# Gate, exponential and sine tiles of the second pair of chunks kept in the space of w2 and h, and a new order of the first thousand operations

## The chip, the core and the metric

The kernel runs on one core of a Trainium2 chip. The metric is the device time of one execution in microseconds; the time of a kernel is the median of its runs. TensorE (PE) multiplies matrices, VectorE (DVE) and ScalarE (ACT) work elementwise, GpSimd (POOL) prepares constants and issues a few transfers, and SyncE (SP) issues nearly all transfers between the main memory and the on-chip memory.

## What is computed

Two blocks follow each other. The first is a gated recurrence with a complex decay, over 768 steps, for 4 batches of 8 heads of width 48; the second mixes the tokens through a low rank and then applies a two-layer perceptron.

```python
mag = np.sqrt(a_re * a_re + a_im * a_im)
scale = np.minimum(mag, 0.999) / (mag + 1e-06)
for t in range(S):                       # S_re, S_im: 48x48 per head
    S_re, S_im = ar * S_re - ai * S_im + kv, ar * S_im + ai * S_re
    y[:, :, t] = einsum(q[:, :, t], S_re)
...
x = y as (batch, seq, heads*48)          # 384 wide
u = x + (x.transpose(0, 2, 1) @ U @ V).transpose(0, 2, 1)
out = u + np.maximum(u @ w_ch1, 0.0) @ w_ch2     # 384 -> 1536 -> 384
```

The weights of the second block (w_ch1, w_ch2, U, V) are given in double precision.

## The kernel before

The 4 x 768 tokens are cut into 24 chunks of 128 tokens (`i`), which are taken in 12 pairs (`g`). For a pair, `gates` loads a_re and a_im (`load_a`, line 527) and makes from them, in the tiles `x`, `y`, `l`, `n`, `ar` and `ai`, the logarithm of the decay and the angle. `within` multiplies the logarithms by a triangle of ones on TensorE (lines 685 and 689) and takes exponentials into `es` and `ef`; `of_blocks` makes totals, which the `totals` transfers bring into the tile `T` (line 711). `turns` and `angles` sum up the angles the same way (lines 788 to 796), and `waves_of` takes cosines and sines into `cs`. In `prep` a chunk's q and k (`load_qkv`, line 534) are multiplied by `es` and `cs` on VectorE and transposed on TensorE (line 851). `chain` then makes the recurrence's output of the chunk from products within blocks (`inner`, `corners`), the running state (`dk`, `G`, `GM`) and their product with the queries (`y`), into `xo`. `mixer` takes two chunks at a time through the second block: `mixed`, `uTp`, `up` (line 1113, 384 to 1536, into `h`) and `down` (1536 to 384).

While this begins, the weights arrive as pairs of 32-bit words in the ring `raw` and are put together to single precision in `single` (lines 555 to 574): w1 first, then U and V, and then w2 in six parts of two rows of blocks each. Up to that time the tile `w2` is empty, and `h` is empty until the first `up`.

In the kernel before, the six gate tiles have one place each (`GATE`, and `GL` for `l`), used by every pair in turn; `es` and `cs` have two buffers each, used by the chunks in turn. Before a pair's a_re and a_im are loaded, the pair before must have read them for the last time.

The program is written as a list of operations with an engine, a kind and the tiles that they read and write (`Plan.add`). The order in which they are issued is not that of the program text: the table `ORDER` gives every operation a place from 0 to 2670, by engine and kind, and `Plan.order` sorts by it. Each engine then works through its own operations in the order of their places and waits where a result is not there yet; the places say nothing else. The table `SPARE` asks, ahead of a place, for a number of cells of idle matmuls, each over 128 columns of the identity (function `idle`, line 1498); they go into a free bank of PSUM, and where none is free they are left out.

Of the kernel before, what the change touches and what calls it, by code (L numbers as in the profile page):

```python
# [10 lines left out]
FP = mybir.dt.float32  # L11
# [7 lines left out]
CH = 128  # L19
# [20 lines left out]
        ("POOL", "load"): {0: [13], 1: [34], 1.5: [28], 2: [16]},  # L40
        ("DVE", "load"): {1: [70]},
# [6 lines left out]
        ("ACT", "gates"): {0: [1, 2, 4, 6, 7, 17, 18, 19, 22, 35, 27, 46, 66, 69], 1: [23, 26, 38, 39, 41, 44, 48, 49, 52, 51, 64, 68], 2: [123, 107,  # L48
# [10 lines left out]
        ("DVE", "gates"): {0: [5, 8, 9, 20, 21, 55, 10], 1: [32, 29, 40, 43, 45, 56, 58], 2: [111, 142, 156, 191, 158], 4: [266, 327, 333, 369, 336],  # L59
# [10 lines left out]
        ("ACT", "angles"): {0: [74, 92, 100, 103, 104], 1: [85, 106, 113, 112, 122], 2: [205, 228, 256, 239, 240, 241, 274, 269, 277], 4: [372, 396,  # L70
# [5 lines left out]
        ("DVE", "angles"): {0: [75, 96], 1: [88, 108], 2: [211, 229, 257], 4: [377, 410, 424], 6: [581, 596, 600, 616, 628, 629, 646], 8: [695, 716,  # L76
# [4 lines left out]
        ("DVE", "prep"): {0: [87, 105, 109], 1: [124, 128, 141], 2: [225, 242, 261], 3: [207, 305, 308], 4: [376, 422, 425], 5: [428, 469, 472], 6:  # L81
# [6 lines left out]
        ("ACT", "prep"): {0: [115, 119, 121, 120], 1: [144, 146, 151, 165], 2: [276, 275, 282, 281], 3: [317, 322, 320, 319], 4: [439, 440, 442, 443],  # L88
# [4 lines left out]
        ("DVE", "rest"): {0: [117, 152, 153, 178, 130, 157, 189], 1: [160, 233, 238, 260, 221, 236, 243, 258], 2: [283, 313, 325, 361, 284, 326, 340,  # L93
# [8 lines left out]
        ("DVE", "levels"): {0: [127, 137, 139, 136, 138, 149], 1: [177, 200, 208, 199, 201, 224], 2: [285, 299, 306, 298, 300, 314], 3: [350, 365,  # L102
# [9 lines left out]
        ("ACT", "levels"): {0: [140], 1: [212], 2: [303], 3: [374], 4: [463], 5: [518], 6: [760], 7: [843], 8: [955], 9: [1009], 10: [1152], 11:  # L112
# [129 lines left out]
def kernel(  # L242
# [28 lines left out]
    DM = H * D  # L271
# [1296 lines left out]
```

## Time and profile before

| | |
|---|---|
| time, median of 3 runs | 629.57 us (629.31 to 633.07) |
| profiled execution | 628.04 us, its span 626.3 us |
| TensorE busy, matmuls | 613.2 us (98%) |
| VectorE busy | 498.8 us (80%) |
| ScalarE busy | 416.4 us (66%) |
| GpSimd busy | 38.4 us (6%) |
| transfers on SP's queue | 39.90 MB, 30.5% of the 16 transfer engines' span |

Matmuls are pipelined and their ends are modelled, and the idle matmuls count as busy; a busy share of TensorE therefore says little where idle matmuls stand. The busy digits of the page are tenths of 40 equal slices of the span. In a list of waits a row gives who waited, for whom, the sum in us, how often, and the longest. Rows of a chain or timeline give the start from the beginning of the span and the length, in us.

### The profile page before, as it was taken

The numbers are of one execution on the slowest core, as the hardware profiler recorded it, in microseconds if no ns is written. First come the engines' busy times: TensorE is split into PE (matmuls) and PEld (weight loads), VectorE is DVE, ScalarE is ACT, GpSimd is POOL, SyncE is SP. The second block draws the span as 40 slices with busy tenths as digits, with TensorE's granted clock in tenths as the row PEclk, the third lists the DMA queues.
The fourth block names the chain that finished last, engine by engine and source line by source line (L and its number), as shares of the span: only waits on it lengthen the run. The fifth ranks groups of instructions, "written<-read, shape, count | busy, mean of one in ns | idle before, by whom it ended". The sixth has DMA issues, their size and how long they took to land.

```text
span 626.3 us, 23516 instructions
## 1 busy us (share of the span) xinstructions
PE 613.2 (98%) x10410; PEld 530.0 (85%) x10410; DVE 498.8 (80%) x887; ACT 416.4 (66%) x807; POOL 38.4 (6%) x79
## 2 busy tenths in 40 slices
PE   7899999999999999999999999999999999999998
PEld 3567778566889889889989989888899998999997
DVE  7999999898899979658877868788889884464554
ACT  7999999998898988687777877688433432202010
POOL 5000000001000010010000100000000100000100
DMA  8965474744334252541413412601203020000101
GB/s 199 203 146 135 108 162 92 181 127 86 55 63 91 37 113 43 100 89 36 91 37 54 105 41 47 134 9 27 60 21 60 14 48 2 1 1 1 45 14 46
DMA packets 173686, 45.76 MB, mean 73 GB/s; under 512 B 167632, under 2 KB 170384, under 8 KB 173584
## 3 DMA queue, kind: packets, MB, share of 16 engines
q1 hardware_dynamic: 171376, 39.90, 30.5%
q0 software_dynamic: 2208, 4.35, 2.1%
q8 instruction: 82, 1.34, 0.9%
q14 instruction: 20, 0.16, 0.1%
HBM read 33.59 MB, written 4.72 MB: 61 GB/s over the span
## 4 chain that ended last, share of the span: by engine, by line
PE 89%; issue 4%; DVE 2%; DMA 2%; ACT 2%; SPq 0%; POOL 0%; DVEq 0%; ACTq 0%; POOLq 0%
PE down L1346 25%; PE up L1113 18%; PE few L1212 11%; PE dk L987 4%; PE tr L851 4%; PE y L1026 4%; PE inner L901 3%; PE y L1018 2%; PE inner L898 2%; PE up L1498 2%; PE tot L733 2%; PE mixed L1080 1%; PE corners L962 1%; PE uTp L1098 1%; PE ph L788 1%
## 5 line engine op out<-in xcount | busy, mean ns | idle before, releaser
L1113 PE MATMUL up<-uT,w 128*128 128x256 f32 x504 | 116.7, 383 | 0.0
L387 DVE TENSOR_TENSOR QK<-QK,T 112x512 f32<-112x512 f32 (+2 forms) x144 | 101.9, 729 | 8.5 <-PE inner L901 4.1
L1113 PEld LDWEIGHTS up<-uT,w 128*128 128x128 f32 x504 | 93.6, 190 | 12.4
L384 ACT ACTIVATE gate<-gate 128x768 f32<-128x768 f32 (+1 forms) x89 | 70.7, 799 | 6.3 <-DVE GS L783 1.7
L1346 PE MATMUL down<-w,h 128*128 128x192 f32 x396 | 72.4, 331 | 0.0
L1346 PEld LDWEIGHTS down<-w,h 128*128 128x128 f32 x396 | 64.1, 190 | 1.5 <-issue 0.7
L862 ACT COPY QK<-tr 112x512 f32<-112x512 f32 x96 | 51.1, 589 | 16.0 <-PE tr L851 15.8
L390 DVE TENSOR_TENSOR xo<-down,xo 128x192 f32<-128x192 f32 (+1 forms) x79 | 29.8, 385 | 27.7 <-PE down L1346 27.3
L387 DVE TENSOR_TENSOR QKC<-qk,cs 128x768 f32<-128x768 f32 x48 | 45.3, 951 | 6.7 <-ACT cs L384 4.3
L1220 ACT COPY h<-few 128x512 f32<-128x512 f32 x30 | 17.2, 586 | 40.8 <-PE few L1212 40.8
L1346 PE MATMUL down<-stage 128*128 128x192 f32 x198 | 37.8, 332 | 0.0
L1102 ACT COPY uT<-uTp 128x384 f32<-128x384 f32 x22 | 10.0, 479 | 41.4 <-PE uTp L1098 26.9
L1212 PE MATMUL few<-gate,w 128*128 128x128 f32 x280 | 34.8, 275 | 0.0
L1288 POOL DMA_DIRECT2D out_dram<-xo x32 | 19.3, 637 | 243.9 <-DVE xo L390 140.6
L1212 PEld LDWEIGHTS few<-gate,w 128*128 128x128 f32 x280 | 33.3, 192 | 0.0
L1346 PEld LDWEIGHTS down<-stage 128*128 128x128 f32 x198 | 32.0, 190 | 0.8 <-issue 0.2
L771 POOL DMA_DIRECT2D gate<-F x15 | 12.3, 820 | 326.8 <-DVE w L572 112.5
L851 PEld LDWEIGHTS tr<-ident,QKC 64*112 64x112 f32 x768 | 24.4, 130 | 9.2 <-issue 5.3
L381 ACT ACT_TABLE_LOAD x24 | 30.8, 1283 | 1.1 <-PEq L1552 0.7
L384 ACT ACTIVATE h<-up 128x512 f32<-128x512 f32 x42 | 24.6, 595 | 9.4 <-PE up L1113 9.0
L967 ACT COPY AT<-corners 32x128 f32<-32x128 f32 x96 | 24.2, 255 | 9.8 <-PE corners L962 8.5
L851 PE MATMUL tr<-ident,QKC 64*112 64x64 f32 x768 | 29.2, 221 | 1.1 <-DVE QKC L387 0.6
(180 smaller groups left out, 1282.9 us busy)
## 6 DMA issues: line engine op xcount, KB each, us to landing
stage<-in_moe_w_ch_dram SPq DMA_DIRECT2D x12, 768.0 KB, 5.1
gate<-in_a_re_dram SPq DMA_DIRECT2D x24, 192.0 KB, 3.1
gate<-in_a_im_dram SPq DMA_DIRECT2D x24, 192.0 KB, 3.7
qk<-in_q_dram SPq DMA_DIRECT2D x24, 192.0 KB, 3.5
VP<-in_v_dram SPq DMA_DIRECT2D x24, 192.0 KB, 3.5
qk<-in_k_dram SPq DMA_DIRECT2D x24, 192.0 KB, 2.8
AT<-DG SPq DMA_DIRECT2D x96, 32.0 KB, 2.6
T<-E SPq DMA_DIRECT2D x48, 48.0 KB, 2.6
```

The source lines that it names most:

```text
L381: ACT(1.37, rank, lambda: nc.scalar.preload_act_table_set(name), writes=[TABLE])
L384: return nc.scalar.activation(out=o, in_=i, func=f, **kw)
L387: nc.vector.tensor_tensor(out=o, in0=a, in1=b, op=OP.mult)
L390: nc.vector.tensor_tensor(out=o, in0=a, in1=b, op=OP.add)
L851: nc.tensor.transpose(out=get(*ps[r])[0:DQ, h], in_=get(*qkc)[at, h].rearrange("p u d -> p (u d)")[:, 0:DQ], identity=ident[at, at], tile_ ...
L862: nc.scalar.copy(out=to, in_=a)
L967: ACT(0.36, RR, lambda r=r, u=u: nc.scalar.copy(out=get(*ATi).rearrange("p (a u) t -> p a u t", u=2)[r:r + BLK, :, u, BLK:2 * BLK], in_=ge ...
L987: nc.tensor.matmul(out=get(*dk[r])[x:end, h], lhsT=get(*ks)[at, h, x // DP, 0:end - x], rhs=get(*VPi)[at, h], start=True, stop=True, tile_ ...
L1026: nc.tensor.matmul(out=get(*y[u])[side(r, u), p], lhsT=k_of(h, r * HC, HC), rhs=get(*(mid_G if r else ("G", i - 1)))[:, h], start=False, s ...
L1113: nc.tensor.matmul(out=get(*ps)[:, e], lhsT=w1[:, f, (ff + e) * 128:(ff + e + 1) * 128], rhs=get(*uT)[:, f], start=(f == 0), stop=(f == KD ...
L1212: nc.tensor.matmul(out=get(*ps)[:, q], lhsT=w()[:, q * 128:(q + 1) * 128], rhs=v[0](), start=(n == 0 and q == 0), stop=True, skip_group_ch ...
L1346: nc.tensor.matmul(out=get(*to)[:, part], lhsT=x(j), rhs=y[:, j], start=(first and j == 0), stop=(j == KH - 1), skip_group_check=not first)
```

## The change

The second pair (`SECOND = (1,)`, chunks 2 and 3) gets places of its own for the six gate tiles: `l`, `ar`, `ai`, `n`, `x` and `y` lie in w2, two rows of blocks each. The cosines and sines (`cs`) and the exponentials (`es`) of chunks 2 and 3 lie in `h`, which becomes one fixed tile, `H_ALL`. The other pairs keep their places and take turns without the second pair. Two waits are written for this: the first step that writes a part of w2 from ScalarE also writes the name `("over", f)`, which shares a ring with the gate tile under it, and the copies of the first mixer's `up` into `h` write the names `("apart", k, ff)` of the tiles under them.

```diff
+    SECOND = (1,)
...
+    H_ALL = singles.tile([128, KF, MC * CH], FP, name="h")
+    APART = ("cs", 2), ("cs", 3), ("es", 2), ("es", 3)
+    apart = [H_ALL.rearrange("p f t -> p (f t)")[:, n * 2 * DM:(n + 1) * 2 * DM] for n in range(4)]
...
-    def single(p, rank, to, o, pieces):
+    def single(p, rank, to, o, pieces, over=()):
...
-                ACT(c_act(n) + 0.1, rank, lambda o_=o_, i_=i_, scale=scale: act(o_(), i_(), AF.Copy, scale=scale), [raw], [at])
+                ACT(c_act(n) + 0.1, rank, lambda o_=o_, i_=i_, scale=scale: act(o_(), i_(), AF.Copy, scale=scale), [raw],
+                    [at] + ([] if to_word else list(over)))
...
-            ring(l, "GL", GL)
+            if g not in SECOND:
+                ring(l, "GL", GL)
...
-            buffer(es, "es", 2, [128, 2, DM])
+            if es not in APART:
+                buffer(es, "es", 2, [128, 2, DM])
...
-                buffer(("cs", i), "cs", 2, [128, H, 2, D])
+                if ("cs", i) not in APART:
+                    buffer(("cs", i), "cs", 2, [128, H, 2, D])
...
-        buffer(h, "h", 1, [128, KF, N])
+        ring(h, "h", [H_ALL])
...
-            ACT(c_act(2 * N) - 0.045, R0, lambda: act(get(*h)[:, ff:ff + 2], get(*ps), AF.Relu if m else AF.Copy), [ps], [h + (ff,)])
+            ACT(c_act(2 * N) - 0.045, R0, lambda: act(get(*h)[:, ff:ff + 2], get(*ps), AF.Relu if m else AF.Copy), [ps],
+                [h + (ff,)] + [("apart", k, ff) for k in range(4) if not m and k * 2 * DM < (ff + 2) * N and (k + 1) * 2 * DM > ff * N])
...
+    for n, nm in enumerate(("l", "ar", "ai", "n", "x", "y")):
+        at = w2[:, 2 * n:2 * n + 2].rearrange("p f m -> p (f m)")
+        if nm[0] == "a":
+            at = at.rearrange("p (c h d) -> p c h d", h=H, d=D)
+        for g in SECOND:
+            ring((nm, g), "h" + nm, [at])
+        ring(("over", 2 * n), "h" + nm, [at])
+    for n, base in enumerate(APART):
+        ring(base, "hs%d" % n, [apart[n]])
+        ring(("apart", n), "hs%d" % n, [apart[n]])
```

`ORDER` and `SPARE` are new. The operations are the same 2671. The lists of places agree from place 1039 on; ahead of it they hold the same operations in another order. Of the lists of the transfers, as an example of how they differ, with the pair of the gates or the chunk in the comment:

```diff
 ("SP", "load")
-   2.5: [89, 80],          # q and k of chunk 1
+   2.5: [56, 97],
-   3: [78, 77, 79, 81],    # a_re and a_im of the second pair
+   3: [33, 77, 80, 95],
-   5.7: [155, 148],        # q and k of chunk 2
+   5.7: [125, 214],
-   7: [364, 405, 335, 302, 246, 206, 195, 202, 222],   # V four times, v of chunk 3, a_re and a_im of the third pair
+   7: [382, 275, 409, 204, 362, 105, 151, 150, 144],
...
-SPARE = {24: 14, 42: 10, 73: 4, 97: 1, 114: 6, 116: 1, 118: 4, 131: 1, 147: 6, 150: 2, 154: 4, ...}
+SPARE = {20: 8, 32: 9, 62: 1, 66: 1, 73: 1, 82: 5, 91: 1, 113: 6, 116: 1, 119: 8, 140: 8, 153: 6, ...}
```

In both programs some of the cells that `SPARE` asks for find no free bank: 107 of 232 are issued in the program before, as 61 matmuls, and 91 of 153 in the changed one, as 46.

More of the change, by code (lines that the diff above doesn't have):

```diff
@@ L39 @@
         25: [1806, 1866, 1822, 1891, 2061], 25.7: [2196, 2082], 26: [2159], 26.7: [2239, 2204], 27: [2345]},
-        ("POOL", "load"): {0: [13], 1: [34], 1.5: [28], 2: [16]},
-        ("DVE", "load"): {1: [70]},
[6 rows of a table removed]
-        ("ACT", "gates"): {0: [1, 2, 4, 6, 7, 17, 18, 19, 22, 35, 27, 46, 66, 69], 1: [23, 26, 38, 39, 41, 44, 48, 49, 52, 51, 64, 68], 2: [123, 107,
[5 rows of a table removed]
+        ("POOL", "load"): {0: [14], 1: [34], 1.5: [84], 2: [31]},
+        ("DVE", "load"): {1: [58]},
[6 rows of a table added]
+        ("ACT", "gates"): {0: [1, 2, 4, 6, 7, 16, 17, 22, 23, 29, 28, 45, 70, 71], 1: [24, 27, 38, 39, 41, 42, 46, 47, 65, 64, 67, 68], 2: [129, 108,
[5 rows of a table added]
         1156, 1161, 1159, 1188, 1160, 1181, 1183, 1216, 1212, 1215, 1246, 1245, 1248, 1241, 1243, 1249], 16: [1298, 1306, 1317, 1315, 1332, 1334,
@@ L58 @@
         1944, 1945, 1951, 1958, 1971, 1987, 1961, 1993, 1994, 1977, 2010, 1999, 1976, 1991, 2003, 2011]},
-        ("DVE", "gates"): {0: [5, 8, 9, 20, 21, 55, 10], 1: [32, 29, 40, 43, 45, 56, 58], 2: [111, 142, 156, 191, 158], 4: [266, 327, 333, 369, 336],
[1 row of a table removed]
+        ("DVE", "gates"): {0: [5, 8, 13, 18, 19, 54, 49], 1: [30, 21, 40, 43, 44, 51, 50], 2: [111, 143, 156, 185, 169], 4: [277, 322, 323, 372, 356],
[1 row of a table added]
         1157, 1178, 1191, 1222], 16: [1326, 1353, 1347, 1352, 1408], 18: [1527, 1537, 1556, 1561, 1604], 20: [1682, 1751, 1719, 1757, 1775], 22:
         [1935, 1957, 1952, 1959, 2005]},
[2 rows of a table removed]
[2 rows of a table added]
         1196, 1244, 1247, 1239, 1242], 16: [1362, 1354, 1391, 1357, 1395, 1379], 18: [1565, 1591, 1579, 1598, 1593, 1573], 20: [1763, 1774, 1782,
         1796, 1794, 1762], 22: [1988, 1974, 1992, 1975, 1983, 2002]},
[2 rows of a table removed]
[2 rows of a table added]
         1608], 20: [1807, 1808, 1894, 1845], 22: [2028, 2186, 2251, 2037]},
-        ("ACT", "angles"): {0: [74, 92, 100, 103, 104], 1: [85, 106, 113, 112, 122], 2: [205, 228, 256, 239, 240, 241, 274, 269, 277], 4: [372, 396,
[2 rows of a table removed]
+        ("ACT", "angles"): {0: [72, 86, 98, 100, 103], 1: [76, 106, 112, 114, 126], 2: [210, 231, 251, 240, 241, 242, 263, 269, 271], 4: [375, 395,
[2 rows of a table added]
         1250, 1194, 1283, 1282], 14: [1265, 1267, 1284, 1293, 1310, 1329, 1386, 1413, 1443, 1398, 1440, 1479], 16: [1409, 1438, 1477, 1498, 1517,
@@ L92 @@
         1912], 20: [2071, 2075, 2099, 2074], 21: [2105, 2111, 2118, 2119], 22: [2278, 2280, 2279, 2270], 23: [2299, 2301, 2303, 2300]},
-        ("DVE", "rest"): {0: [117, 152, 153, 178, 130, 157, 189], 1: [160, 233, 238, 260, 221, 236, 243, 258], 2: [283, 313, 325, 361, 284, 326, 340,
[2 rows of a table removed]
+        ("DVE", "rest"): {0: [118, 149, 155, 175, 159, 170, 194], 1: [174, 229, 234, 259, 209, 235, 248, 253], 2: [288, 315, 325, 366, 291, 314, 324,
[2 rows of a table added]
         1041, 1074, 1071, 1078, 1079, 1083], 10: [1100, 1164, 1170, 1195, 1090, 1118, 1217, 1221], 11: [1136, 1168, 1176, 1218, 1234, 1238], 12:
@@ L101 @@
         2314, 2375], 23: [2363, 2365, 2368, 2381, 2400, 2401]},
-        ("DVE", "levels"): {0: [127, 137, 139, 136, 138, 149], 1: [177, 200, 208, 199, 201, 224], 2: [285, 299, 306, 298, 300, 314], 3: [350, 365,
[2 rows of a table removed]
+        ("DVE", "levels"): {0: [123, 135, 148, 136, 137, 152], 1: [177, 192, 202, 195, 198, 225], 2: [292, 302, 308, 301, 303, 312], 3: [328, 371,
[2 rows of a table added]
         [1134, 1154, 1162, 1147, 1149, 1169], 12: [1324, 1360, 1370, 1343, 1355, 1389], 13: [1330, 1364, 1365, 1342, 1346, 1394], 14: [1528, 1547,
@@ L126 @@
         2290, 2382, 2384, 2383], 23: [2385, 2386, 2408, 2410, 2409]},
-        ("ACT", "rest"): {0: [185, 184, 182, 183, 216, 214, 215], 1: [263, 265, 267, 264, 280, 279, 278], 2: [355, 347, 343, 344, 380, 384, 385], 3:
[2 rows of a table removed]
+        ("ACT", "rest"): {0: [191, 182, 200, 201, 219, 223, 222], 1: [255, 261, 256, 258, 280, 279, 278], 2: [342, 341, 336, 335, 385, 390, 391], 3:
[2 rows of a table added]
         1105], 10: [1210, 1193, 1211, 1208, 1237, 1240, 1236], 11: [1224, 1225, 1209, 1229, 1261, 1263, 1264], 12: [1439, 1436, 1418, 1428, 1454,
@@ L134 @@
         2217, 2234, 2296, 2293, 2295], 22: [2378, 2374, 2373, 2372, 2395, 2393, 2392], 23: [2397, 2376, 2396, 2394, 2411, 2413, 2414]},
[1 row of a table removed]
[1 row of a table added]
         1287], 4: [1411, 1501, 1468], 5: [1603, 1625, 1673], 6: [1872, 1897, 1920, 1917], 7: [2048, 2112, 2114], 8: [2193, 2226, 2236], 9: [2419,
         2423, 2429, 2430], 10: [2475, 2498, 2501], 11: [2553, 2568, 2572]},
-        ("ACT", "small"): {0: [594, 291, 330, 498, 421, 557, 592, 605, 620, 631], 1: [746, 809, 769, 817, 788, 849, 845], 2: [989, 985, 1088, 1139,
[1 row of a table removed]
+        ("ACT", "small"): {0: [595, 285, 307, 492, 396, 554, 590, 549, 623, 636], 1: [744, 791, 777, 807, 782, 856, 859], 2: [984, 978, 1088, 1139,
[1 row of a table added]
         [1643, 1680, 1736, 1758, 1700, 1780, 1744, 1740], 6: [1875, 1921, 1919, 1965, 1962, 1937, 2022, 1990, 2016], 7: [2126, 2124, 2139, 2144, 2148,
@@ L142 @@
         2504, 2513, 2519, 2523, 2537, 2527, 2532], 11: [2582, 2580, 2592, 2595, 2600, 2611, 2597, 2616]},
-        ("DVE", "small"): {0: [232, 598, 632, 640, 638, 639, 685, 668, 601, 611, 728, 740], 1: [708, 741, 694, 830, 832, 844, 869, 898, 894, 925, 910,
[1 row of a table removed]
+        ("DVE", "small"): {0: [246, 600, 631, 637, 640, 638, 685, 682, 603, 607, 731, 737], 1: [705, 741, 690, 817, 843, 844, 870, 871, 889, 913, 912,
[1 row of a table added]
         1281], 3: [1279, 1285, 1366, 1368, 1367, 1425, 1407, 1433, 1445, 1447, 1432, 1452, 1434, 1488, 1462, 1484, 1510], 4: [1435, 1412, 1560, 1562,
@@ L168 @@
         2651, 2653, 2657, 2658, 2659, 2660, 2667, 2668]},
-        ("POOL", "small"): {0: [819, 875], 1: [1119, 1116, 1117], 2: [1337, 1278, 1338], 3: [1670, 1446, 1515], 4: [1778, 1776, 1777], 5: [2049, 1855,
+        ("POOL", "small"): {0: [932, 933], 1: [1119, 1116, 1117], 2: [1337, 1278, 1338], 3: [1670, 1446, 1515], 4: [1778, 1776, 1777], 5: [2049, 1855,
         2008], 6: [2154, 2101, 2162], 7: [2343, 2276, 2342], 8: [2633, 2632, 2648], 9: [2629, 2634, 2663], 10: [2635, 2627, 2636]},
-        ("POOL", "angles"): {6: [618], 8: [705, 744], 10: [870, 923], 12: [1097], 14: [1273, 1302], 16: [1472, 1516], 18: [1669], 20: [1879, 1913],
+        ("POOL", "angles"): {6: [615], 8: [708, 733], 10: [882, 931], 12: [1097], 14: [1273, 1302], 16: [1472, 1516], 18: [1669], 20: [1879, 1913],
         22: [2039, 2077]},
@@ L174 @@
 }
-SPARE = {24: 14, 42: 10, 73: 4, 97: 1, 114: 6, 116: 1, 118: 4, 131: 1, 147: 6, 150: 2, 154: 4, 168: 1, 171: 3, 186: 1, 193: 3, 194: 2, 213: 1, 259: 6,
[3 rows of a table removed]
+SPARE = {20: 8, 32: 9, 62: 1, 66: 1, 73: 1, 82: 5, 91: 1, 113: 6, 116: 1, 119: 8, 140: 8, 153: 6, 157: 4, 167: 1, 168: 1, 207: 6, 216: 1, 217: 1, 282:
+         1, 352: 2, 436: 1, 514: 5, 518: 5, 527: 4, 546: 4, 547: 25, 551: 12, 596: 2, 601: 1, 606: 3, 624: 1, 632: 3, 646: 1, 653: 1, 664: 1, 672: 2,
+         678: 5, 694: 1, 695: 1, 717: 1, 718: 2}
 class Plan:
@@ L420 @@
     V = singles.tile([128, S], FP, name="V")
+    H_ALL = singles.tile([128, KF, MC * CH], FP, name="h")
+    APART = ("cs", 2), ("cs", 3), ("es", 2), ("es", 3)
+    apart = [H_ALL.rearrange("p f t -> p (f t)")[:, n * 2 * DM:(n + 1) * 2 * DM] for n in range(4)]
+    apart = [a.rearrange("p (h u d) -> p h u d", u=2, d=D) if n < 2 else a.rearrange("p (u m) -> p u m", u=2) for n, a in enumerate(apart)]
     def column(nm, value):
@@ L596, in weights @@
             single(p, ("w2", f), ("w2", f), w2[:, f:f + 2].rearrange("p f m -> p (f m)"),
-                   [tokens(moe_w_ch2[f * 128:(f + 2) * 128])])
+                   [tokens(moe_w_ch2[f * 128:(f + 2) * 128])], [("over", f)])
             p += 1
@@ L1442 @@
         for g in range(NG if nm in AREA else 0):
-            ring((nm, g), "g" + nm, [AREA[nm]])
+            if g not in SECOND:
+                ring((nm, g), "g" + nm, [AREA[nm]])
         if nm == "ef":
```

8 lines of the change are left out of this document (4 added, 4 removed), and 101 rows, old and new, of tables (ORDER, SPARE).

## The prediction

> **What bounds the kernel now.** I read the page's busy shares and slices first, then the busy times by stretch, with stretches cut where the order of the program changes character, and then who waited for whom.
>
> ```profile
> span 626.3 us, 23516 instructions
> PE 613.2 (98%) x10410; PEld 530.0 (85%) x10410; DVE 498.8 (80%) x887; ACT 416.4 (66%) x807; POOL 38.4 (6%) x79
> ...
> PE   7899999999999999999999999999999999999998
> ...
> DVE  7999999898899979658877868788889884464554
> ACT  7999999998898988687777877688433432202010
> ```
>
> The whole-span shares say TensorE. The stretches say something else for the part that the change touches:
>
> ```profile
> core 0: us, PE busy (x) PEld busy (x) DVE busy (x) ACT busy (x) POOL busy (x), PEclk, DMA share, GB/s
> 5.10:20.00 14.90, 10.76 (x60) 5.95 (x60) 13.02 (x28) 12.65 (x27) 5.39 (x20) 1.00 0.96 230
> 20.00:72.00 52.00, 49.53 (x1084) 34.85 (x1087) 50.76 (x82) 50.40 (x95) 0.00 (x0) 1.00 0.66 152
> 72.00:100.00 28.00, 27.87 (x775) 22.20 (x765) 27.36 (x43) 27.17 (x53) 0.00 (x0) 1.00 0.52 110
> 100.00:213.00 113.00, 111.60 (x1849) 88.92 (x1839) 103.72 (x166) 101.62 (x187) 5.63 (x7) 1.00 0.42 95
> 213.00:313.00 100.00, 99.86 (x1934) 88.19 (x1927) 78.34 (x132) 79.83 (x157) 7.11 (x11) 1.00 0.40 79
> 313.00:600.00 287.00, 286.64 (x4588) 264.80 (x4587) 211.88 (x405) 141.26 (x288) 15.17 (x25) 1.00 0.19 39
> ```
>
> From 5.1 to 100 us VectorE works 91.14 of 94.90 us and ScalarE 90.22: these two set the pace, and TensorE's 88.16 is padded. The padding is the idle matmuls of line 1498; the busy times of that line alone, summed over 0 to 313 us, are
>
> ```profile
> sum 313.00, PE 36.42 PEld 22.07; mean PE 6.07 PEld 3.68
> ```
>
> From 213 us on TensorE is never free (99.86 of 100, 286.64 of 287) and has no padding, so whatever the front gains or loses there arrives at the end unchanged, as long as VectorE and ScalarE keep up, and they have 20 us of slack in the 100 after 213.
>
> **The change, part by part.** The two orders hold the same operations, and their lists of places are equal from place 1039 on, which runs at about 213 us. Ahead of it stand, in both, 314 VectorE and 364 ScalarE instructions. None is added, removed or resized, except idle matmuls. So the sum of the work up to that point is fixed, and only idle time can go. VectorE's idle time is 14.90 - 13.02 = 1.88, 52.00 - 50.76 = 1.24, 28.00 - 27.36 = 0.64 and 113.00 - 103.72 = 9.28 us: 13.04 us in all, the ceiling of any gain. ScalarE has 16.06 by the same subtraction. Who ended VectorE's waits between 5 and 213 us:
>
> ```profile
> DVE gate L638 <- ACT gate L384: 2.6, 3, 1.9
> DVE xo L390 <- PE mixed L1080: 1.9, 2, 1.3
> DVE F L799 <- ACT F L384: 1.0, 2, 0.9
> DVE qk L387 <- DMA qk<-in_k_dram: 0.8, 1, 0.8
> DVE GS L666 <- ACT GS L663: 0.8, 1, 0.8
> DVE gate L390 <- ACT gate L384: 0.8, 1, 0.8
> ...
> DVE qk L387 <- DMA qk<-in_q_dram: 0.4, 1, 0.4
> ```
>
> (The 1.9 of the first row ends at 5.1, so 0.7 of it counts here.) Loads account for 1.2 us, and no row names a gate tile's load. What the new places set free is the waiting of SP's queue for gate tiles, whose rows are small, while its long waits are for other buffers, which the change leaves alone:
>
> ```profile
> SPq L534 <- DVE QKC L387: 17.3, 4, 7.0
> ...
> SPq L527 <- DVE gate L387: 1.3, 1, 1.3
> ```
>
> *Tiles moved.* Gate tiles of the second pair in w2, its exponentials and sines in h: no instruction's size changes, so 0 by itself. Each gets a new wait. The first copy of each w2 part waits until the gate tile under it was last read. The first such copy ran at 100.23 us, and the second pair's phase products, which read the last of those tiles, ended by 51.8 (51.09 and 0.66): 48 us of cover. The copies of the first `up` products into h wait until the sines and exponentials of chunks 2 and 3 were last read. The tightest is `up` at 66.19, whose copy starts after it ends at 68.98, while the last sines had been used when the transposes at 65.16 began: 3.8 us of cover. Were it gone, ScalarE's next instructions would wait, and TensorE for them; each us late would cost a us at most. Both at 0.
>
> ```profile
> 100.23 0.92 ACT L384 ACTIVATE w<-stage 128x768 f32<-128x768 f32 x1
> ```
>
> ```profile
> 51.09 0.66 PE ph L793 x2
> ...
> 65.16 1.04 PE tr L851 x32
> 66.19 2.79 PE up L1113 x12
> ```
>
> *Order of the front, to 100 us.* I count close handoffs: an instruction that needs a result of another engine with less than 0.8 us of its own engine's work placed between that result and itself (durations from this trace, places from the order tables). In places 0 to 349 VectorE has 30 of them before and 23 after, ScalarE 34 and 34, TensorE 31 and 30. If VectorE's 3.76 us of idle time up to 100 us shrink in proportion, the gain is 3.76 x 7/30 = 0.9. The other reading is the padding: idle matmuls stand where a wait of TensorE is expected, and ahead of place 505 they fall from 89 cells of 128 columns to 73 (107 to 91 in all). At 36.42/107 = 0.34 us a cell that is 5.4 us of expected waiting less, but VectorE has only 3.76 to give. Ends 0 and -3.76; I take **-2.0**, about halfway, since both readings point the same way.
>
> *Order from 100 to 213 us.* Close handoffs in places 350 to 1043: VectorE 39 to 49, ScalarE 59 to 57, TensorE 35 to 27; 133 and 133. By VectorE alone the 9.28 us would become 9.28 x 49/39 = 11.66 (+2.4); by the other two, 94 to 84, they would become 8.3 (-1.0). Ends -4.6 (half of the idle time) and +7 (ten more stalls of 0.7, the mean of the rows above); I take **0**, by the equal total.
>
> *Loads moved.* SP's queue is in order. Loads of the third pair's gates move from places 195-222 to 105-151, one load of the second pair from 78 to 33, q of chunk 1 from 89 to 56; v of chunk 0 goes from 53 to 83, of chunk 1 from 125 to 176, and k of chunk 2 from 148 to 214, behind a copy of the totals that waits for ScalarE.
>
> ```profile
> 44.16 1.25 SPq L711 DMA_DIRECT2D T<-E  x2
> ```
>
> ```profile
> 47.66 0.95 DVE L387 TENSOR_TENSOR qk<-qk,es 128x768 f32<-128x768 f32 x1
> ```
>
> ```profile
> qk<-in_k_dram SPq DMA_DIRECT2D x24, 192.0 KB, 2.8
> ```
>
> That copy was issued at 44.16 and takes 0.6 of the queue; k of chunk 2 goes out behind it at about 44.8 and lands 2.8 later, at 47.6. VectorE used it at 47.66, and wants it 0 to 2 us earlier now. Queued behind that product are VectorE's `w` and `F` steps, and the transposes of chunk 2. Ends 0 and +1.5, taken **+0.3**. The weights' second part has one 192 KB load more ahead of it: 0.85 us at the 230 GB/s of the first row; ends 0 and +0.85, taken **+0.2**. The q and k of chunk 3, which were late by 0.4, are no longer behind the queue's long wait: 0 to -0.4, counted in the order above. On GpSimd's queue the preparation of two constants moves, ahead of its use as before, five additions of angles move by 3 to 12 places either way, and two stores of the output, which nobody reads, go behind three of these: 0.
>
> *Padding at the start.* Ahead of the first sums, 14 cells become 8 (chain of instructions on TensorE in order of time).
>
> ```profile
> 1.42 6.10 PE L1498 MATMUL tr<-ident 128*128 128x384 f32 x10 [1.42 <-POOL ident masks.py:199]
> 8.86 0.88 PE L689 MATMUL es ps<-GL,mid 128*128 128x384 f32 x2 [1.34 <-DVE GL L390]
> 9.58 2.32 PE L1498 MATMUL tr<-ident 128*128 128x384 f32 x8
> ```
>
> The 14 cells took 6.10 us, 0.436 each; the 10 after 9.58 took 2.32, 0.232 each: TensorE starts slow and is up to speed by then. Eight cells at 0.436 end at 4.9 and leave 4.0 us empty before 8.86. If TensorE is slow again there, the two sums of three cells each take 3 x 0.436 = 1.31 for 0.88 and 0.81. Ends 0 and +0.9, taken **+0.3**, because VectorE has other work there.
>
> *Sum.* -2.0 + 0 + 0.3 + 0.2 + 0.3 = -1.2 us. The profiled execution took 628.04 us (span 626.3 and 1.74 around it), so 626.8. It lies 1.5 under the median of the runs, 629.57; on that scale the forecast is **628.4 us**, with 625 to 632 as its own range.
>
> [...]
>
> **Rivals.** *The idle time closes.* For: the sum of the work allows 13.04 us, and a free choice of places could use it. Against: handoffs are as close as before from 100 us on, where 9.28 of it lies. Half to three quarters of it: -6.5 to -9.8, about 621.5 us.
>
> *Close handoffs stall VectorE between 100 and 213 us.* Ten more than before, all of them in places 700 to 1043; each that stalls costs 0.7. It decides from two stalls on, which eat the 1.2. Five: 628.4 + 3.5 = 631.9; all ten: 635.4. For: VectorE is at 92% there, and what it loses TensorE cannot make up. Against: TensorE has eight fewer.
>
> *The change does nothing.* The tiles cover loads that nobody waits for and the new order is worth the old one: 629.6.
>
> [...]
>
> **How the numbers follow.** Forecast 0.47, nothing 0.16, stalls 0.22, idle time closed 0.12, slow TensorE 0.03. About 1% is what a measurement of this kernel can tell from no change: 623.3 to 635.9. Faster by more: three quarters of the closed case, 0.09. Slower by more: a third of the stalls, which run on past ten, and the slow TensorE, 0.11. Within: 0.80. The range goes from the middle of the closed case, 621.5, to the full stalls, 635.4.
>
> **What would show it.** Right: VectorE's idle time from 5.1 us to place 1039 between 10 and 14 us, less than 3 of it ahead of place 505; no wait of VectorE for k of chunk 2 above 1.5; no wait at the first copies into w2 and h. Wrong: place 1039 reached more than 6 us off 213; TensorE idle or padded after 213; cells of the padding at 0.4 us after 20 us; any new row of VectorE waiting for a load above 2 us.

## The result, and the profile after

In the comparison of the two kernels the changed kernel took 628.17 us (median of 22 runs, 626.90 to 631.15) and the kernel before 630.15 (22 runs, 628.46 to 633.17): a ratio of 0.9965, 95% interval 0.9952 to 0.9979, and medians 2.0 us apart. The forecast was 628.4 us, within 1% with a chance of 0.80. A second comparison of the same two kernels, among the experiments below, gave 0.9941 (0.9921 to 0.9962). The kernel before moved more between comparisons (medians 630.15, 632.70, 631.97 and 632.04) than the kernel after (628.17 and 628.31). Medians and ranges here and below leave out a run that lies more than 1.5% above the fastest of its kernel; there is one, of e7 (635.83 us).

The page of the profile after, and its busy times by the stretches that the prediction used (columns: length of the stretch, busy us and instructions of PE, PEld, DVE, ACT and POOL, granted clock, DMA share, GB/s):

```profile
span 627.0 us, 23447 instructions
PE 609.9 (97%) x10380; PEld 526.2 (84%) x10380; DVE 499.7 (80%) x887; ACT 415.8 (66%) x807; POOL 38.1 (6%) x79
...
PEclk7999999999999999999999999999999999999999
```

```profile
5.10:20.00 14.90, 10.54 (x55) 6.53 (x56) 11.71 (x26) 11.06 (x24) 5.74 (x20) 0.77 0.97 242
20.00:72.00 52.00, 49.09 (x1115) 34.85 (x1114) 51.13 (x82) 50.72 (x96) 0.00 (x0) 1.00 0.59 141
72.00:100.00 28.00, 24.41 (x619) 18.20 (x618) 27.10 (x43) 27.32 (x54) 0.00 (x0) 1.00 0.54 122
100.00:213.00 113.00, 111.70 (x1882) 88.29 (x1880) 104.81 (x166) 101.64 (x186) 5.16 (x7) 1.00 0.43 96
213.00:313.00 100.00, 99.81 (x1956) 87.95 (x1956) 79.21 (x135) 80.28 (x159) 7.15 (x11) 1.00 0.40 79
313.00:600.00 287.00, 286.80 (x4589) 264.83 (x4590) 211.45 (x405) 141.50 (x288) 15.20 (x25) 1.00 0.19 39
```

This profiled execution took 628.76 us and the one before 628.04: the pair of traces shows a loss of 0.7 us where the medians show a gain of 2.0. The profiled execution of before was one of its quickest (its other runs reach down to 627.76 and up to 637.86), the one of after a little above its median. VectorE's idle time in the four stretches, 3.19 + 0.87 + 0.90 + 8.19 = 13.15 us, is that of before (13.04) with another distribution: 1.31 us more ahead of 20 us, 1.09 less behind 100. Idle time is not the whole of it: VectorE reaches place 1039 at 212.6 us in before and at 213.7 in after, and from 5.1 us to there it works 194.46 and 195.44 us. The same operations took VectorE 1.0 us more in the new order, which the prediction's "the sum of the work up to that point is fixed" did not allow; why is not shown.

```profile
5.10:212.60 207.50, 199.35 (x3711) 151.57 (x3714) 194.46 (x314) 191.46 (x357) 11.02 (x27) 1.00 0.53 121
```

```profile
5.10:213.70 208.60, 196.44 (x3700) 148.53 (x3700) 195.44 (x314) 191.44 (x359) 10.90 (x27) 0.98 0.52 121
```

So the pair points at two things, a slower start and fewer stalls from 100 us on. One trace of each cannot tell which of them recur; that has to come from further runs.

The start is on TensorE's timeline (start, length, instruction, and in brackets its idle time and who ended it):

```profile
1.42 3.58 PE L1519 MATMUL tr<-ident 128*128 128x384 f32 x6 [1.42 <-POOL ident masks.py:199]
8.79 1.62 PE L696 MATMUL es ps<-GL,mid 128*128 128x384 f32 x2 [3.79 <-DVE GL L390]
10.21 4.05 PE L1519 MATMUL tr<-ident 128*128 128x384 f32 x6
14.05 1.25 PE L696 MATMUL ef ps<-GL,fore 128*128 128x384 f32 x2
```

The eight cells of padding take 3.58 us (0.45 each) and end at 5.0, TensorE is empty for 3.79 us, and the first sum then takes 1.62 us where before it took 0.88; the nine cells behind it take 0.45 us each instead of 0.232. VectorE's first product of q and k of chunk 0 starts at 21.45 (before 19.57).

Who ended VectorE's waits between 5 and 213 us, and the long wait of SP's queue up to 110 us:

```profile
DVE gate L387 <- ACT gate L384: 2.5, 2, 1.4
DVE gate L645 <- ACT gate L384: 2.4, 2, 2.1
DVE xo L390 <- PE mixed L1089: 1.6, 2, 1.1
DVE F L807 <- ACT F L384: 1.2, 2, 0.9
...
DVE gate L647 <- DMA gate<-in_a_re_dram: 0.5, 1, 0.5
...
DVE GS L790 <- DMA gate<-F: 0.2, 1, 0.2
```

```profile
SPq L539 <- DVE QKC L387: 7.8, 3, 3.7
```

No row names a load of q or k any more (before 0.8 and 0.4 us), none names w2 or h, and SP's queue stands 7.8 us for `QKC` up to 110 us instead of 17.3 (up to 213 us, 23.7 instead of 27.1).

### The profile page after: what moved, and what is told of

Its sections match the earlier page's. It is cut to its first block, busy times and chain, and to the rows that moved or that the text cites. A ratio compares the mean times of both kernels' runs of the same rounds, so it can differ in the third digit from the quotient of the medians.

```text
span 627.0 us, 23447 instructions
## 1 busy us (share of the span) xinstructions
PE 609.9 (97%) x10380; PEld 526.2 (84%) x10380; DVE 499.7 (80%) x887; ACT 415.8 (66%) x807; POOL 38.1 (6%) x79
## 4 chain that ended last, share of the span: by engine, by line
PE 77%; ACT 4%; DVE 3%; DMA 1%; issue 1%; SPq 0%; ACTq 0%; DVEq 0%
PE down L1356 24%; PE up L1122 15%; PE few L1222 11%; PE dk L996 3%; PE tr L860 3%; PE y L1035 3%; PE inner L910 2%; PE down L1313 2%; PE inner L907 2%; PE tot L741 2%; PE y L1027 2%; PE mixed L1089 2%; PE es ps L692 1%; PE ef ps L692 1%; PE uTp L1107 1%; PE corners L971 1%
## 5 line engine op out<-in xcount | busy, mean ns | idle before, releaser
L387 DVE TENSOR_TENSOR QK<-QK,T 112x512 f32<-112x512 f32 (+2 forms) x144 | 102.1, 732 | 8.4 <-PE inner L910 4.3
L384 ACT ACTIVATE gate<-gate 128x768 f32<-128x768 f32 (+1 forms) x82 | 64.8, 795 | 7.4 <-DVE GS L791 3.2
L387 DVE TENSOR_TENSOR QKC<-qk,cs 128x768 f32<-128x768 f32 x44 | 41.7, 955 | 6.3 <-ACT cs L384 3.6
```

Of the source, the lines that this page charges most:

```text
L384: return nc.scalar.activation(out=o, in_=i, func=f, **kw)
L387: nc.vector.tensor_tensor(out=o, in0=a, in1=b, op=OP.mult)
```

## The experiments

Twelve kernels ran, in three groups; kernels of one group share their runs of the kernel before. Time differences between two kernels of a group are differences of medians, with a 95% interval from resampling the runs. The ratios are not quotients of the two medians; these can differ (for e2 0.9942 beside 0.9923, for e12 0.9935 beside 0.9951), so a difference of a few tenths of a per cent between two ratios says little.

| kernel | median us (runs, lowest to highest) | ratio to before, 95% interval |
|---|---|---|
| group 1, before 632.70 (29) | | |
| e1 tiles only | 633.05 (12, 630.3 to 634.8) | 0.9997, 0.9973 to 1.002 |
| e2 start padding 14 and 10 | 629.05 (6, 626.8 to 629.3) | 0.9923, 0.9902 to 0.9944 |
| e3 new front, old rest | 630.77 (12, 628.9 to 634.3) | 0.9959, 0.9937 to 0.9981 |
| e4 old front, new rest | 630.90 (12, 628.1 to 634.7) | 0.9966, 0.9941 to 0.9991 |
| group 2, before 631.97 (35) | | |
| e5 start padding 22 and 12 | 627.85 (12, 626.2 to 631.0) | 0.9935, 0.9905 to 0.9964 |
| e6 no start padding | 629.07 (12, 627.3 to 631.2) | 0.9949, 0.992 to 0.9977 |
| e7 no padding behind place 160 | 629.25 (11, 626.3 to 631.6) | 0.9945, 0.9914 to 0.9975 |
| e8 before, again | 631.84 (8, 627.8 to 633.3) | 0.9985, 0.995 to 1.002 |
| group 3, before 632.04 (27) | | |
| e9 before, w2 combined early | 630.80 (12, 628.5 to 633.6) | 0.9983, 0.9956 to 1.0009 |
| e10 new front padded, old rest | 629.18 (12, 628.2 to 630.9) | 0.9956, 0.9939 to 0.9974 |
| e11 after, again | 628.31 (6, 627.3 to 628.8) | 0.9941, 0.9921 to 0.9962 |
| e12 start padding 14 and 10, again | 627.94 (10, 627.0 to 630.6) | 0.9951, 0.9927 to 0.9976 |

### e1: the tiles without the order

```diff
-ORDER, SPARE = the tables of after
+ORDER, SPARE = the tables of before      # tiles in w2 and h stay as in after
```

> The tiles of the second pair lie in w2 and h, as in the changed kernel, but all 2671 operations keep the places, and the idle matmuls the cells, of the kernel before. Theory 'the order does it': the tiles free nothing that anybody waited for, so the ratio to the kernel before is 1.000 (within 0.0015), and the idle time of VectorE from 5.1 to 213 us stays at 12 to 14 us. Rival 'the tiles do it': fewer waits in SP's queue let loads start earlier, and the ratio is that of the changed kernel, 0.9965, or most of it.

Measured: 633.05 us, 0.9997 (0.9973 to 1.002). The tiles alone show no gain, so the gain comes with the order. The expectation on VectorE failed: its idle time from 5.1 to 213 us was 16.94 us and not 12 to 14. The repeated trace of before (e8) has 14.98 there, so part of that is not the tiles' doing; that the tiles cost nothing is not shown.

### e3 and e4: one half of the order each

```diff
 e3: places 0 to 504 as in after,  then the rest in the sequence of before
 e4: places 0 to 504 as in before, then the rest in the sequence of after
```

> The changed kernel's tiles; its first 505 places and their idle matmuls, and from there on all other operations in the sequence of the kernel before, with its idle matmuls. If the gain of the changed kernel comes from the order ahead of place 505 (about 100 us), the ratio to the kernel before is 0.9965 or lower; if it comes from the order between 505 and 1039, the ratio is 1.000 or somewhat above it, because the slow start remains (up to 1.003).

> The complement: the first 505 places and their idle matmuls of the kernel before, all other operations in the sequence of the changed kernel with its idle matmuls. If the gain comes from ahead of place 505, the ratio to the kernel before is 1.000; if it comes from 505 to 1039, it is 0.9965 or, without the slow start, 0.993 to 0.996. If each half gives a part, both this and the other half-and-half lie between 0.997 and 0.999.

Measured: 630.77 and 630.90 us. Against e1, which differs from each by that half alone, the new front brings -2.3 us (-3.7 to -0.4), with the slow start in it, and the new rest -2.2 us (-4.1 to -0.7). Both halves gain. They need not add up: the whole order against e1, by way of before (ratios 0.9965 or 0.9941 against 0.9997), comes to 2.0 to 3.5 us, less than the 4.4 of the halves but inside their intervals. In e1's own group the closest to the whole order is e2 below, with longer padding at the start: 4.0 us less than e1 (-6.4 to -2.8). By their ratios alone e3 (0.9959) and e4 (0.9966) would each have the whole gain, and the two expectations have no case for that.

The traces say more on the second half than on the first. VectorE's idle time, in us, in each trace, cut where it reaches places 505 and 1039:

| order, trace | 5.1 us to place 505 | place 505 to 1039 |
|---|---|---|
| old front, old rest: before, e8, e1, e9 | 3.76, 3.86, 6.05, 4.57 | 9.28, 11.12, 10.90, 9.69 |
| new front, old rest: e3, e10 | 4.14, 3.47 | 11.36, 10.20 |
| old front, new rest: e4 | 6.10 | 8.09 |
| new front, new rest: after, e11 | 5.00, 4.11 | 8.15, 8.52 |
| the same, start padding 14 and 10 or 22 and 12: e2, e12, e7, e5 | 2.67, 3.46, 2.96, 3.14 | 8.42, 8.09, 7.40, 8.43 |
| the same, no start padding: e6 | 6.42 | 7.99 |

With the new rest VectorE stands 7.4 to 8.5 us behind place 505, with the old 9.3 to 11.4, and the two do not overlap. One wait goes with the order in all of these traces: ScalarE's conversion of the angles (`GS`) waits for GpSimd's additions `gate<-F`. From 100 to 215 us it stands 0.9 to 2.9 us for them in the six traces with the old rest and not at all in the eight with the new. The last of these additions in before, e3 and after (start, length, and in brackets the wait):

```profile
190.00 0.78 POOL L771 DMA_DIRECT2D gate<-F  x1 [7.55 <-DVE F L799]
193.39 0.51 ACT L780 CAST GS<-gate 128x384 fp32r<-128x384 f32 x1 [0.89 <-DMA gate<-F]
```

```profile
191.25 0.78 POOL L779 DMA_DIRECT2D gate<-F  x1 [7.66 <-DVE F L807]
196.02 0.51 ACT L788 CAST GS<-gate 128x384 fp32r<-128x384 f32 x1 [2.27 <-DMA gate<-F]
```

```profile
190.04 0.76 POOL L779 DMA_DIRECT2D gate<-F  x1 [7.43 <-DVE F L807]
194.18 0.51 ACT L788 CAST GS<-gate 128x384 fp32r<-128x384 f32 x1
```

In the new order ScalarE comes to the conversion 4.1 us after the addition is issued, and the addition is there. VectorE takes over from the conversion: `GS` waits of VectorE for ScalarE's `GS` are 2.3 us in e3, 0.7 in before and 0.3 in after. No run moves this instruction alone, so its share of the gain is not measured. On the front the traces show no such gap between old and new.

### e2, e5, e6: padding ahead of the first sums

```diff
-SPARE = {20: 8, 32: 9, 62: 1, ...}
+SPARE = {20: 14, 32: 10, 62: 1, ...}     # e2 and e12
+SPARE = {20: 22, 32: 12, 62: 1, ...}     # e5
+SPARE = {62: 1, ...}                     # e6
```

> The changed kernel, with 14 and 10 cells of idle matmuls ahead of the first two sums, as the kernel before has them, in place of 8 and 9. Theory 'slow clock at the start': the sums es ps and ef ps of chunk 0 take 0.88 and 0.81 us again in place of 1.62 and 1.25, the granted clock from 5 to 20 us is 1.00, and the time falls by 0.5 to 2 us against the changed kernel: ratio to the kernel before 0.993 to 0.9955. Rival 'VectorE has other work there': the sums are fast again but the ratio stays at 0.9965 within 0.0007.

> The changed kernel with 22 and 12 cells of idle matmuls ahead of the first two sums, where e2 has 14 and 10. Theory 'slow clock at the start': the cells now reach up to the first sum, so that it always finds the full clock; once the clock is up a cell takes 0.23 us, so the padding ends before 9.5 us and delays the first sum by 0.5 us at most. Ratio to the kernel before 0.991 to 0.994, and less spread between runs than e2. Rival 'too much padding': the first sum waits for the idle matmuls, and the ratio is worse than that of e2 (0.9923) by 0.001 to 0.003.

> The changed kernel with no idle matmuls ahead of the first two sums. Theory 'slow clock at the start': all TensorE work up to some 20 us runs at the slow clock, the first sums take 1.3 to 1.6 us each, and the ratio to the kernel before is 0.997 to 1.001, as slow as the changed kernel or slower. Rival 'VectorE has other work there, and the idle matmuls themselves hold up the first sums': the ratio is 0.994 or lower.

The starts of e2, e5 and e6 on TensorE's timeline, in this order:

```profile
8.51 0.88 PE L696 MATMUL es ps<-GL,mid 128*128 128x384 f32 x2 [1.65 <-DVE GL L390]
9.23 2.32 PE L1519 MATMUL tr<-ident 128*128 128x384 f32 x8
```

```profile
1.42 7.31 PE L1519 MATMUL tr<-ident 128*128 128x384 f32 x16 [1.42 <-POOL ident masks.py:199]
8.59 0.88 PE L696 MATMUL es ps<-GL,mid 128*128 128x384 f32 x2
```

```profile
8.55 1.62 PE L696 MATMUL es ps<-GL,mid 128*128 128x384 f32 x2 [8.55 <-DVE GL L390]
9.96 1.49 PE L696 MATMUL ef ps<-GL,fore 128*128 128x384 f32 x2
```

With a gap of 1.65 us (e2) or none (e5) the first sum takes 0.88 us, and in e2 the padding behind it 2.32 us for 10 cells; without any padding (e6) the early sums are slow one after the other, 1.62, 1.49, 1.65 and 1.49 us. In the traces VectorE's first product of chunk 0 starts at 19.0 (e2), 19.3 (e5) and 21.6 us (e6). In time, from no padding to 22 and 12 cells is -1.2 us (-2.1 to -0.1). Of the expectations, e2's theory held in the trace (0.88 and 0.81 us, clock 1.00), and its ratio of 0.9923 fell below the 0.993 to 0.9955 named. e5's 0.9935 lies where both its theory and its rival put it; its first sum was not delayed (8.59 against 8.51), and its runs spread over 4.8 us, not less than e2's 2.4. e6's 0.9949 lies between its theory and its rival. e2's ratio to before (0.9923) lay clear of the 0.9965 of after, but those two came from different groups, so both kernels were run again side by side (e11, e12).

### e11 and e12: after and its padded form side by side

> The kernel after, unchanged, on the same chip as the next. Theory that its clock at the start is slow in each execution, since the gap of some 4 us ahead of the first sum is in its order: es 1.6 us, ef 1.25 us or more, first product of q and k of chunk 0 at 21 to 21.6, ratio 0.995 to 0.998. Rival, that the slow start was a thing of the one profiled execution: es 0.88, product at 19 to 19.6, and ratio as for the padded kernel, 0.992 to 0.9945.

> The kernel after with 14 and 10 cells of padding at the start in place of 8 and 9, a second time, beside the kernel after itself. Theory that the padding alone is worth some 2 us: median 1.5 to 2.6 us below that of the kernel after in the same call, ratio to before 0.991 to 0.9945. Rival, that the difference seen earlier came from comparing runs of two calls: within 0.7 us of the kernel after.

The starts of e11 and e12:

```profile
8.92 1.62 PE L696 MATMUL es ps<-GL,mid 128*128 128x384 f32 x2 [3.71 <-DVE GL L390]
10.33 3.78 PE L1519 MATMUL tr<-ident 128*128 128x384 f32 x6
```

```profile
8.44 0.89 PE L696 MATMUL es ps<-GL,mid 128*128 128x384 f32 x2 [0.91 <-DVE GL L390]
9.16 2.32 PE L1519 MATMUL tr<-ident 128*128 128x384 f32 x8
```

The slow start belongs to the order of after with its eight cells: it came again, behind the same gap of 3.7 us (and in e3, which shares that front, behind 3.4), though the second sum took 0.81 us and the first product came at 20.9. e11's ratio, 0.9941, lies where the rival put it all the same. But its price in time did not repeat: 628.31 against 627.94, a difference of -0.4 us (-1.0 to +1.3). The expected 1.5 to 2.6 us failed; the rival of e12, within 0.7 us, fits. The spans of the two pairs of profiled executions differ by 1.9 (627.0 and 625.1) and 1.0 us (626.6 and 625.6). What is shown is that the start is slow and that VectorE's first products are later for it, by 1.0 us in the second pair (20.9 and 19.95) and 2.4 in the first (21.45 and 19.0); that the padding is worth more than about 1 us in time is not shown.

### e7: no idle matmuls behind place 160

```diff
-SPARE = {20: 8, 32: 9, ..., 153: 6, 157: 4, 167: 1, ..., 718: 2}
+SPARE = {20: 14, 32: 10, ..., 153: 6, 157: 4}
```

> e2 (14 and 10 cells at the start) without any idle matmul behind place 160 (about 37 us). [...] Rival 'slow TensorE': somewhere between 37 and 150 us matmuls take twice their time, and the ratio rises by 0.003 or more.

```profile
20.00:72.00 52.00, 47.20 (x1100) 32.89 (x1099) 51.57 (x83) 51.06 (x98) 0.00 (x0) 1.00 0.63 147
72.00:100.00 28.00, 24.56 (x712) 18.75 (x711) 27.74 (x44) 27.68 (x54) 0.00 (x0) 1.00 0.58 141
100.00:213.00 113.00, 109.93 (x1858) 86.25 (x1858) 105.06 (x166) 102.88 (x188) 5.16 (x7) 1.00 0.41 89
```

Measured: 629.25 us, 0.9945 (0.9914 to 0.9975), 0.0022 above the 0.9923 of e2 and short of the 0.003 from which the rival counts; the interval takes in both. In the profiled execution the granted clock is 1.00 in each of these stretches, and VectorE is as busy as with the padding (184.37 us of the three together, 183.11 in e2). Other executions were not as good: two of the eleven, 630.47 and 631.58 us, show a mean granted clock of 0.989, and the run left out 0.983, while none of the 40 runs of e2, e5, e6 and e12 is below 0.994. So one execution did without this padding; that all can is not shown.

### e8 and e9: where the kernel before loses its time

> The kernel before once more, for a second profile of it. Its first profile, at 628.04 us, was among the fastest of its runs. If the slow clock at the start explains the spread of its runs, this profile, should it be slower by 2 us or more, has eight cells of idle matmuls ahead of the second sum that take about 4 us in place of 2.3, and VectorE is late by 1 to 2 us from there to the end; if transfers explain it, VectorE or ScalarE waits longer for a load.

The repeated run of before had a quick start and a span of 631.1 us, 4.8 more than the first profile. VectorE is level with the first profile up to place 503 (+0.2 us), 2.0 us behind at 139 us, and 4.3 behind at 418. The two losses, ScalarE's waits from 100 to 142 us and TensorE's wait at 398 us:

```profile
ACT w L384 <- DMA stage<-in_moe_w_ch_dram: 2.1, 2, 1.2
```

```profile
120.85 0.90 ACT L384 ACTIVATE w<-stage 128x768 f32<-128x768 f32 x1 [1.19 <-DMA stage<-in_moe_w_ch_dram]
...
126.01 0.89 ACT L384 ACTIVATE w<-stage 128x768 f32<-128x768 f32 x1 [0.94 <-DMA stage<-in_moe_w_ch_dram]
```

```profile
398.43 0.79 PE L1018 MATMUL y<-VP,AT 64*64 64x48 f32 x32 [1.60 <-DMA AT<-DG]
```

Both are transfers that land late: parts of w2, and a block of `DG` copied into `AT`. The first profile of before has neither row, and those of after, e2, e11 and e12 have neither; e1, which has the order of before too, has both (1.4 us in one wait and 1.4 in two). e3 and e10, with the old rest, have no wait for w2. So what sets these two executions of before apart is how late such transfers land, not the start, which was the other branch of the expectation.

It is not all that spreads the runs of before. Both traces have a granted clock of 1.00, and over the 91 runs of before in the three groups time goes with the clock: the 25 runs at 1.000 have a median of 631.06 us, the 31 at 0.997 632.20, and the 13 at 0.992 or less 635.77. The 22 runs of after show no such link (628.24 at 1.000, 627.85 below it). No execution of before at a low clock was profiled, so whether the low clock or the delay comes first stays open. The gain is there without it: in group 3 the runs at 1.000 have medians of 631.31 (before, 5 runs) and 628.43 us (e11, 2 runs).

The loads of w2 wait for a staging tile, which `w<-stage,w` (L574) of an earlier part releases. The order of after runs this instruction right behind the conversion before it, the order of before 2.6 and 3.8 us later. e9 moves only these two instructions:

```diff
-        ("DVE", "w2"): {0: [547, 549, 567], 2: [569, 579, 597], ...
+        ("DVE", "w2"): {0: [547, 549, 550], 2: [569, 579, 580], ...
```

> The order of before, and its tiles, with two instructions of VectorE moved: the combining of the first two parts of w2 (L574, `w<-stage,w`) comes right behind the conversion before it, as in the order of after, where before ran it 2.6 us (at 111.54) and 3.8 us (at 117.62) later. These two release the staging tiles into which the next two parts of w2 are loaded. Theory that the old order between 100 and 142 us loses its time to these two loads (in the repeated run of before ScalarE waited 1.2 us and 0.9 us for them at 120.9 and 126.0, and VectorE stood 2.0 us later at 139 us): the loads start some 2 to 3 us earlier, no wait of ScalarE for `stage<-in_moe_w_ch_dram` in the profile, and the median falls by 1 to 2 us: ratio 0.997 to 0.9985. Rival, that the new order between 100 and 213 us gains elsewhere, and that these waits only take up time that is lost anyway: ratio 0.999 to 1.001, with the waits gone or not.

```profile
ACT w L384 <- DMA stage<-in_moe_w_ch_dram: 0.2, 1, 0.2
```

Measured: 630.80 us, 0.9983 (0.9956 to 1.0009). The wait is 0.2 us in the profile, where e8 had 2.1 and the first profile of before none; the time lies where the first theory wants it, and the interval still takes in the rival. Inconclusive.

### e10: the padded front with the old rest

```diff
 places 0 to 504 as in after, the rest as in before
-SPARE = {20: 8, 32: 9, ...}
+SPARE = {20: 14, 32: 10, ...}
```

> The first 505 places in the order of after and the rest in the order of before, with the padding at the start at 14 and 10 cells in place of 8 and 9. Theory that the slow clock at the start hid the larger part of what the new front brings: the first sums take 0.88 and 0.81 us instead of 1.62 and 1.25, the first product of q and k of chunk 0 comes at 19.0 to 19.6 us instead of 20.8, and the ratio to before falls from 0.996 to 0.992 - 0.9945. Rival, that what is lost at the start is idle time again by 100 us: ratio 0.995 to 0.997 as without the padding.

Measured: 629.18 us, 0.9956 (0.9939 to 0.9974), where the same without the padding (e3) had 0.9959: nearer the rival, although the first sums did come down to 0.88 us and the first product to 19.6. The interval reaches into the theory's range too, and by the medians of their groups e10 gains 2.9 us and e3 1.9, so the padding's worth on this front is not settled. Against e11 in the same group the new rest is worth -0.9 us (-2.2 to -0.3), even with the slow start on the side of after.

## Why the prediction was right, and where it was not

The result is close to the forecast, 628.2 against 628.4 us, but not by all of its own terms, and in part by luck.

- **Tiles moved, 0:** as far as shown, right. e1 is level with before within its interval, and neither the copies into w2 nor those into h wait in after. In the two traces with these tiles and the old front (e1, e4) VectorE idles 6.0 and 6.1 us ahead of place 505, in the three without the tiles 3.8 to 4.6; why is open.
- **Order of the front, -2.0:** right in size, not shown in its mechanism. The new first half measured -2.3 us against e1 (-3.7 to -0.4) with the slow start in it. The term said that VectorE's idle time ahead of 100 us would shrink. With the start padding as it is, it did not: 5.00, 4.11 and 4.14 us with the new front, 3.76 and 3.86 in the two traces of before; only with longer start padding is it 2.67 to 3.47. VectorE reaches place 505 at 102.1 us in after, at 102.0 in before, and at 99.6 in e2.
- **Order from 100 to 213 us, 0:** the step that failed. Its measured size is -2.2 us (-4.1 to -0.7) by e4 against e1, and -0.9 (-2.2 to -0.3) by e11 against e10. The term was read from a count of close handoffs, 133 on both sides, and VectorE's ten more did not stall: its idle time from place 505 to 1039 is 9.3 to 11.4 us in the traces with the old rest and 7.4 to 8.5 with the new. The count left out transfers. The old order has ScalarE wait 0.9 to 2.9 us for GpSimd's additions, which the prediction put at 0, and in two executions 1.4 and 2.1 us for parts of w2; the new order has neither wait. How much of the term is the one or the other stays open: e9 took the wait for w2 away and could not show its worth in time, and nothing moved the other alone.
- **k of chunk 2, +0.3, and the weights' second part, +0.2:** 0 each in the trace of after. No wait for either is left, and the 0.8 and 0.4 us that before waited for k and q are gone.
- **Start padding, +0.3 between 0 and 0.9:** the slow start came as priced or more; its reason is not settled. The sums took 1.62 and 1.25 us for 0.88 and 0.81, 1.2 us more, above the upper end of 0.9 in the trace. The prediction priced a TensorE that is slow again behind the empty 4.0 us. But the eight cells ahead of the gap still took 0.45 us each, so nothing shows that TensorE had come up to speed when the gap began, and without any cells (e6) the first sum takes 1.62 us as well. That TensorE starts slow is shown (0.45 us a cell, where in before ten behind the first sum take 0.232 each); what the gap of 3.79 us did here is not. The price in time, 0.4 us (-1.3 to +1.0) by e11 and e12, is compatible with +0.3 and with the end.

So the sum of -1.2 was too small by 0.8 to 2.5 us, mostly by the middle term. That the absolute forecast fits is partly luck in the scale: it started from the 629.57 us of the runs shown, and later groups gave 630.2 to 632.7 for before.

**The rivals.** "The change does nothing": excluded by the interval up to 0.9979. "Close handoffs stall VectorE": no such rows, and e4 gains. "The idle time closes": no, VectorE's 13.04 us of idle time are 13.15 in after, and 10.4 to 14.4 in the other traces of the new order. A slow TensorE, 0.03 among the chances: in after it shows at the start only, where the second sum at 14.05 us (1.25 us) is the last slow one, and without start padding (e6) like instructions are slow up to some 22 us (`ph` 2.77 us at 19.47, in after 1.46 at 19.03). e7, with no padding from place 160 on, keeps a clock of 1.00 from 20 to 213 us in its trace, but some of its runs have a low mean clock (0.983 and twice 0.989).

**What was to be seen.** VectorE's idle time between 10 and 14 us: 13.15, yes. Less than 3 of it ahead of place 505: no, 4.96 already up to 100 us, because of the slow start (1.20 + 0.59 + 0.88 = 2.67 in e2, from the rows below). Place 1039 was reached at 213.7 us (before 212.6), TensorE works 286.80 of 287 us behind 313, no wait of VectorE for a load exceeds 0.5 us up to there, and slow cells stand only ahead of 15 us (nine from 10.21 us take 4.05 us, six from 24.55 us 1.45).

```profile
5.10:20.00 14.90, 12.19 (x69) 7.18 (x68) 13.70 (x29) 12.91 (x27) 6.78 (x20) 1.00 1.03 253
20.00:72.00 52.00, 48.77 (x1114) 34.81 (x1114) 51.41 (x82) 50.81 (x97) 0.00 (x0) 1.00 0.62 147
72.00:100.00 28.00, 24.76 (x714) 19.18 (x714) 27.12 (x43) 27.49 (x52) 0.00 (x0) 1.00 0.53 132
```

No version is shown to beat the kernel after: e5 and e12 have the lowest medians, 627.85 and 627.94 us, and e12's lead over after is inside its interval.

## What to carry to other kernels

Where a change is worth a few tenths of a per cent, one trace of each side can point the wrong way: profile the kernel before a second time, look for the waits that go with the order in every trace, and set the times of all runs beside their granted clocks. When an order is judged by its handoffs between engines, count the transfers asked for just in time as handoffs too. A slow instruction that a trace shows early, here 1.0 to 2.4 us on VectorE, is not yet a loss of the same size in the median; run both forms side by side.

## What the runs showed of the hardware

At the start a cell of the idle matmuls takes 0.42 to 0.47 us (mean of the eight and of the nine cells in after, e3 and e11) or 0.232 (the ten behind the first sum in before, e2, e4, e8, e10 and e12), and the first sum 1.62 or 0.88. Two things go with it, the number of cells ahead and the length of TensorE's gap before the first sum, and the runs do not part them fully.

With no cells (e6), or eight cells that all ran slow (after, e11, e3; gaps of 3.4 to 3.8 us), the first sum took 1.62 us. With 14 cells a gap of 0.91, 0.97, 1.34, 1.53 or 1.65 us (e12, e10, before, e4, e2) left the sums at 0.88 to 0.89 us; at 1.97 to 2.00 us (e9, e1, e7) the speed was lost in or right behind the sum. But the repeated run of before (e8) kept it across a gap of 2.90 us. So the length of the gap alone does not decide it. e7, e9 and e8, all with 14 cells ahead of the gap:

```profile
8.68 1.47 PE L694 MATMUL es ps<-GL,mid 128*128 128x384 f32 x2 [2.00 <-DVE GL L388]
9.94 3.47 PE L1517 MATMUL tr<-ident 128*128 128x384 f32 x8
```

```profile
9.07 0.99 PE L689 MATMUL es ps<-GL,mid 128*128 128x384 f32 x2 [1.97 <-DVE GL L390]
9.86 3.95 PE L1498 MATMUL tr<-ident 128*128 128x384 f32 x8
```

```profile
9.33 0.88 PE L689 MATMUL es ps<-GL,mid 128*128 128x384 f32 x2 [2.90 <-DVE GL L390]
10.05 2.32 PE L1498 MATMUL tr<-ident 128*128 128x384 f32 x8
```

Nor does the time of the cells ahead of the gap decide it alone: the 14 took 5.68, 6.07 and 5.25 us in e9, e1 and e7, where the speed was lost, and 5.02 in e8, 5.44 in e2 and 6.10 in before, where it was kept. In e12 a later gap of 1.88 us, behind a sum of 0.81 us, left the next sum quick (0.91). e9 has the front of before unchanged, so that front, with its 14 cells, loses speed at the start in some executions as well (3.95 us for the ten cells behind the first sum, 2.32 in before). The granted clock does not always show it: in e11 the stretch from 5.1 to 20 us reads 1.00, with a first sum of 1.62 us. The durations of like instructions are the surer reading.

```profile
5.10:20.00 14.90, 10.52 (x58) 6.59 (x58) 12.30 (x26) 11.54 (x25) 5.85 (x20) 1.00 0.94 236
```
